# Block-causal attention and a gated MLP on one core: moves of turned P first on SyncE's queue, values loaded from ScalarE's queue, two diagonal copies on GpSimd

## The chip, the cores and the metric

The kernel runs on one core of one Trainium2 chip. The metric is the time of an execution on the device in microseconds (us); lower is better. Five engines are named as in the profile: PE (TensorE), DVE (VectorE), ACT (ScalarE), POOL (GpSimd) and SP (SyncE, which only issues transfers here). PEld is the loading of weights into PE. Transfers are also issued by ACT and POOL; an issuing engine's queue is shown as SPq, ACTq or as a DMA row of POOL.

## What is computed

Attention over 8 batches, 8 heads, 576 positions and 64 channels, with a mask of blocks of 64, and then a gated MLP over all 4608 rows of 512 features.

```python
scores = scale * np.matmul(q, k.transpose(0, 1, 3, 2))
mask = (pos[:, None] // 64) >= (pos[None, :] // 64)
scores = np.where(mask, scores, -1000000000.0)
scores = scores - np.max(scores, axis=-1, keepdims=True)
attn = np.exp(scores)
attn = attn / (np.sum(attn, axis=-1, keepdims=True) + 1e-09)
x = np.matmul(attn, v)            # then (B, H, S, D) -> (B * S, H * D)
...
gate = 1.0 / (1.0 + np.exp(-(x @ w_gate)))
val = x @ w_val
return (gate * val @ w_out).astype(np.float32)
```

All inputs are float32. Products that need more than one pass of PE's fast float format are made from a high and a low part (names in H and L).

## The kernel before, in words

**Stages.** The work runs over 32 pairs (a batch and two heads each, p = 0 to 31). Pairs 0 to 7 are laid out by a script (`FRONT`), in which every engine's order is written by hand. Pairs 8 to 31 run in a loop over p, in which the steps of table `REST` are written one after the other; a scheduler puts each engine's instructions into an order, within the limits that `behind` sets (an order between two instructions without a wait). Between the steps, `places` ticks deal out matmuls of the MLP's first part (`mlp`), which uses the rows of batches that are complete. After the loop comes the rest of the MLP, which the change does not touch.

**One pair.** Step `s` makes the scores of four row blocks into PSUM tiles named bank, and for each a maximum (nm, DVE) and two exps (ACT); `t` does the same for the last 64 rows (the tail). For pairs 8 to 30 (`moved`) exp writes P into a tile Z or XB, which take turns from pair to pair; both are called Zc. P must be transposed before it is multiplied with the values. DVE turns 32 x 32 blocks in place (`turn`, steps `tr3`, `tr2`, and the last and largest piece in `trm`). Step `trm` (`move`) then carries the blocks between the four groups of 32 partitions into tile G: twelve transfers of 100 KB, six issued by POOL and six by SP, and four copies on ACT for the blocks that stay in their group (the diagonal).

**The product with values** (`av`) of a pair is written into the next pair's loop pass, at step `AV`: 44 matmuls read G and the values VS, and DVE multiplies the result by rb, which gives xT. `finish` follows: XH (ACT), a store of xT to DRAM (ACT's queue) and XL (POOL). rb holds the reciprocals of the sums (step `r`, `recip`): DVE makes rT, four small transfers write it to DRAM (r_d), and three read it back over 64 partitions each (rb).

**Loads.** In pass p, steps `k` and `q` load pair p + 3 into tile rqk, four transfers of 72 KB each, and at the end of the pass the values of pair p + 2 are loaded into VS by three transfers. All go over SP's queue, as do r_d, rb and half of the moves. Step `k` also starts the preparation of the next pair (`prep`): DVE turns rqk into KQ, ACT makes KH and QH, POOL KL and the small copies QBH and QBL for the tail.

Names and lines before: `issue` L291 (its transfers are all L292), `load` L294, `turn` L580 (L583), `move` L585 (moves L589, copies L592), exps L486 and L530, xT L664, `finish` L788 (XH L790, store L793, XL L795), the loop L1193.

## Time and profile before

| what | before |
|---|---|
| median of 3 executions | 1152.83 us (1152.31 to 1154.24) |
| profiled execution | 1156.51 us, span 1154.7 us |
| PE busy | 1101.6 us, 95% of the span |
| DVE busy | 847.1 us, 73% |
| ACT busy | 621.6 us, 54% |
| POOL busy | 431.4 us, 37% |
| SP's transfers (q1) | 143.90 MB, 46.8% of 16 engines' span |
| granted PE clock, mean | 0.989 |

A busy PE is one with a matmul under way, whose end is modelled, so 95% does not say that PE works at its peak. The busy shares are means over stages that differ. SP has no busy time of its own in the profile; how full its queue is has to be read from its issues in order of time.

### The profile page before, as it was taken

The page shows a single profiled execution, that of the slowest core. Times are in us where ns is not written, and L with a number is a line of the kernel's source. Part 1 is how long each engine was busy: PE and PEld are TensorE (multiplying, and loading weights), DVE is VectorE, ACT ScalarE, POOL GpSimd, SP SyncE. Part 2 cuts the span into 40 slices and gives each one's busy share as a digit, 9 for nine tenths or more (in the row PEclk, how much of TensorE's full clock was granted, in tenths as well). Part 3 has the DMA queues.
Part 4 walks back from the last instruction along what each step waited for, and adds up shares of the span by engine and source line. Part 5 has one row for each costly group of instructions (what it writes and reads, how often), then busy time and mean ns, then how long its engine had stood idle before and what let it go on. Part 6 is the DMA issues. An engine that isn't in the chain of part 4 may idle for free.

```text
span 1154.7 us, 19512 instructions
## 1 busy us (share of the span) xinstructions
PE 1101.6 (95%) x6593; PEld 940.8 (81%) x6593; DVE 847.1 (73%) x1482; ACT 621.6 (54%) x1344; POOL 431.4 (37%) x560
## 2 busy tenths in 40 slices
PE   8999898988988998979999999999999999999998
PEld 6677676776766676767889999899899999998998
DVE  7999886776767677648869975776886665756754
ACT  6887776767767777744335354444553332422421
POOL 3655355444635555331011304213124243263250
PEclk9999999999999999999999999999999999999999
DMA  8797578778878887754412335505388345254351
GB/s 167 173 184 164 144 172 198 167 159 204 169 182 169 203 184 160 184 160 133 156 38 81 110 118 198 174 36 210 111 317 298 135 137 183 70 187 130 108 164 55
DMA packets 270691, 181.63 MB, mean 157 GB/s; under 512 B 204576, under 2 KB 225312, under 8 KB 269952
## 3 DMA queue, kind: packets, MB, share of 16 engines
q1 hardware_dynamic: 248080, 143.90, 46.8%
q10 hardware_dynamic: 17712, 21.30, 5.8%
q0 software_dynamic: 4800, 15.19, 5.5%
q8 instruction: 52, 0.85, 0.3%
q14 instruction: 47, 0.39, 0.1%
HBM read 104.73 MB, written 47.33 MB: 132 GB/s over the span
## 4 chain that ended last, share of the span: by engine, by line
PE 64%; DMA 11%; DVE 9%; SPq 6%; ACT 5%; issue 4%; POOL 1%; ACTq 0%; DVEq 0%; POOLq 0%
PE b L1250 30%; PE m L1320 11%; PE b L1320 6%; PE bank L347 5%; PE m L179 4%; SPq L292 4%; PE m L188 3%; PE bank L179 3%; ACT G L592 3%; DVE nm L474 2%; DMA G<-XB 2%; DMA rb<-r_d 2%; DMA r_d<-rT 2%; SPq L589 2%; DVE XB L583 1%
## 5 line engine op out<-in xcount | busy, mean ns | idle before, releaser
L1250 PE MATMUL b<-XH,w 128*128 128x384 f32 x1344 | 349.1, 335 | 0.3 <-ACT t L899 0.3
L1250 PEld LDWEIGHTS b<-XH,w 128*128 128x128 f32 x1344 | 243.8, 188 | 4.3 <-ACT t L899 0.7
L1250 PE MATMUL b<-XL,w 128*128 128x384 f32 x672 | 223.5, 335 | 0.0
L1250 PEld LDWEIGHTS b<-XL,w 128*128 128x128 f32 x672 | 126.1, 188 | 1.7
L347 PE MATMUL bank<-G,VS 128*64 128x64 f32 (+3 forms) x1264 | 103.6, 319 | 22.5 <-DMA r_d<-rT 9.4
L1320 PE MATMUL m<-wo,hH 128*128 128x512 f32 x368 | 119.9, 391 | 0.0
L347 PEld LDWEIGHTS bank<-G,VS 128*64 128x64 f32 x1264 | 73.2, 145 | 50.6 <-issue 14.0
L1069 POOL TENSOR_TENSOR XB<-XB 128x384 f32<-128x384 f32 x20 | 22.3, 1116 | 238.1 <-DMA XB<-xT_d 139.9
L188 PE MATMUL m<-wo,hH 128*128 128x512 f32 x256 | 85.7, 398 | 8.1 <-ACT ost L899 6.0
L1273 ACT ACTIVATE g<-g 128x384 f32<-128x384 f32 x72 | 37.9, 526 | 93.3 <-DVE g L1286 49.3
L179 PE MATMUL m<-XH,wg 128*128 128x512 f32 x240 | 81.5, 397 | 4.4 <-ACT t L203 4.4
L1082 ACT CAST XH<-XB 128x1536 fp32r<-128x1536 f32 (+2 forms) x72 | 65.1, 941 | 36.1 <-DVE XB L1080 23.5
L474 DVE TENSOR_REDUCE nm<-bank 128x2 f32<-128x1024 f32 (+1 forms) x96 | 77.0, 803 | 7.1 <-ACT Z L486 5.5
L179 PE MATMUL m<-XH,wv 128*128 128x512 f32 x240 | 81.7, 398 | 0.0
L1320 PEld LDWEIGHTS m<-wo,hH 128*128 128x128 f32 x368 | 69.0, 188 | 13.0
L1083 DVE TENSOR_TENSOR XL<-XB,XH 128x1536 fp32r<-128x1536 f32 (+2 forms) x72 | 75.8, 1085 | 0.0
L1320 PE MATMUL m<-wo,hL 128*128 128x512 f32 x184 | 72.1, 392 | 0.0
L1320 PE MATMUL b<-wo,hH 128*128 128x512 f32 (+1 forms) x216 | 71.5, 383 | 0.0
L486 ACT ACTIVATE Z<-bank,nm 128x512 f32<-128x512 f32 (+3 forms) x104 | 53.5, 530 | 30.8 <-DMA G<-XB 18.4
L389 POOL TENSOR_SCALAR KQ<-KQ 128x128 f32<-128x128 f32 x28 | 16.8, 601 | 131.7 <-DVE KQ L377 127.2
L188 PEld LDWEIGHTS m<-wo,hH 128*128 128x128 f32 x256 | 48.1, 188 | 20.9 <-ACT ost L899 8.1
L486 ACT ACTIVATE XB<-bank,nm 128x512 f32<-128x512 f32 (+3 forms) x88 | 45.4, 531 | 24.5 <-DMA G<-Z 13.6
(215 smaller groups left out, 2553.8 us busy)
## 6 DMA issues: line engine op xcount, KB each, us to landing
pr<-part_d SPq DMA_DIRECT2D x66, 256.0 KB
xT_d<-xT ACTq DMA_DIRECT2D x32, 288.0 KB
XB<-xT_d SPq DMA_DIRECT2D x16, 576.0 KB
part_d<-pr SPq DMA_DIRECT2D x36, 256.0 KB
rqk<-in_q_dram SPq DMA_DIRECT2D x120, 72.0 KB
rqk<-in_k_dram SPq DMA_DIRECT2D x120, 72.0 KB
out_dram<-pr SPq DMA_DIRECT2D x33, 256.0 KB
part_d<-ost ACTq DMA_DIRECT2D x32, 256.0 KB
```

What stands on the lines that cost most here:

```text
L179: mm = nc.tensor.matmul(ps, lhsT=lh, rhs=rh, start=(i == 0), stop=(i == n - 1))
L188: mm = nc.tensor.matmul(ps, lhsT=lh[:, f, t * P:(t + 1) * P], rhs=rh, start=(f == i == 0), stop=(f == F1 - 1 and i == 2))
L292: return pin(engine_of(queue), queue.dma_start(**kw), True)
L347: pe_last[:] = [pin("PE", nc.tensor.matmul(*args, **kw)).ins]
L474: mark("DVE", nc.vector.tensor_reduce(out=nm_()[:, c0:c0 + 2], in_=ps[:, :, c:c + n], axis=AX.X, op=ALU.max, negate=True))
L486: mark("ACT", nc.scalar.activation(out=dst, in_=src, func=AF.Exp, bias=nm_()[:, c0 + h:c0 + h + 1], accum_out=sm[:, 5 * h + i:5 * h + i + 1]))
L592: mark("ACT", nc.scalar.copy(out=Gc[q, c], in_=Zc[q, c]))
L1082: nc.scalar.copy(out=XO[j][0][:, a:b], in_=x)
L1083: sub = nc.vector.tensor_sub(out=XO[j][1][:, a:b], in0=x, in1=XO[j][0][:, a:b].bitcast(F32))
L1250: mm = nc.tensor.matmul(ps, lhsT=lh, rhs=rh, start=(first and k == 0), stop=(k == n - 1), skip_group_check=not first)
L1273: mark2("ACT", nc.scalar.activation(out=t, in_=c, func=AF.Tanh, scale=0.5))
L1320: mm = nc.tensor.matmul(po[t][:, cols], lhsT=lh[:, f, t * P:(t + 1) * P], rhs=wo[:, f, e, cols], start=((whole or half == 0) and i == 0), ...
```

## The change

Five edits go together.

- Six of the twelve moves are issued by SP as before, and are now marked; every later transfer that `issue` puts on SP's queue is placed behind the last marked move.
- Steps `k` and `q` no longer issue one load each: both loads are issued at step `q`, which is written behind `trm` and `r`.
- The loads of values go to ACT's queue.
- Of the four diagonal copies, two go to POOL, behind POOL's six moves.
- `finish` is a step of its own (`fin`) behind `trm` for passes 8 to 30; XH is placed behind ACT's last G copy and XL behind POOL's. The MLP matmuls of a completed batch are added at that step too.

```diff
--- before.py
+++ after.py
@@ -22,7 +22,7 @@
 AHEAD = 3
 KEEP = 32
 
-REST = (("s", 3), ("t", 1), ("AV", 2), ("tr3", 1), ("tr2", 1), ("k", 0), ("trm", 0), ("r", 0), ("q", 0), ("trl", 2), ("trt", 2))
+REST = (("s", 3), ("t", 1), ("AV", 2), ("tr3", 1), ("tr2", 1), ("k", 0), ("trm", 0), ("fin", 0), ("r", 0), ("q", 0), ("trl", 2), ("trt", 2))
 NB = 25
 B_OF = {2: (0, 3), 3: (6, 4), 0: (14, 1), 1: (16, 2)}
 LT = 14
@@ -289,7 +289,10 @@
         nc.gpsimd.memset(p_tile(4)[:, S:], 0.0)
 
         def issue(queue, **kw):
-            return pin(engine_of(queue), queue.dma_start(**kw), True)
+            ins = queue.dma_start(**kw)
+            if queue is nc.sync and "moves" in last:
+                behind(ins.ins, last["moves"])
+            return pin(engine_of(queue), ins, True)
 
         def load(p, what, queue=nc.sync, part=None):
             b, hp = pairs[p]
@@ -586,10 +589,15 @@
 
                 turn(LT, NB)
                 for k, (c, a) in enumerate(itertools.permutations(range(4), 2)):
-                    (nc.sync if k % 2 else nc.gpsimd).dma_start(out=Gc[32 * c:32 * c + 32, a], in_=Zc[32 * a:32 * a + 32, c])
+                    ins = (nc.sync if k % 2 else nc.gpsimd).dma_start(out=Gc[32 * c:32 * c + 32, a], in_=Zc[32 * a:32 * a + 32, c])
+                    mark("moves" if k % 2 else "POOL", ins)
                 for c in range(4):
                     q = slice(32 * c, 32 * c + 32)
-                    mark("ACT", nc.scalar.copy(out=Gc[q, c], in_=Zc[q, c]))
+                    if c % 2:
+                        ins = nc.gpsimd.tensor_copy(out=Gc[q, c], in_=Zc[q, c])
+                        behind(ins.ins, last["POOL"])
+                    else:
+                        mark("ACT", nc.scalar.copy(out=Gc[q, c], in_=Zc[q, c]))
 
             def tr_main(i):
                 if moved:
@@ -792,7 +800,10 @@
                     mark("ACT", cut)
                 nc.scalar.dma_start(
                     out=xT_d[b, hp * P:(hp + 1) * P, :], in_=xT_())
-                nc.gpsimd.tensor_sub(out=XL[:, hp], in0=xT_(), in1=XH[:, hp].bitcast(F32))
+                low = nc.gpsimd.tensor_sub(out=XL[:, hp], in0=xT_(), in1=XH[:, hp].bitcast(F32))
+                if "POOL" in last and p < len(pairs) - 2:
+                    behind(low.ins, last["POOL"])
+                    behind(cut.ins, last["ACT"])
 
             def step(what, is_fine=False, alt=False, queue=nc.sync):
                 if is_fine:
@@ -814,9 +825,10 @@
                     tr_low()
                 elif what == "trt":
                     tr_tail()
+                elif what == "fin":
+                    finish()
                 else:
                     av()
-                    finish()
 
             return step
 
@@ -1199,16 +1211,19 @@
                 if what == "AV":
                     if prev:
                         prev("av")
-                    if prev and what == "AV" and pairs[p - 1][1] == NP - 1:
-                        pb = pairs[p - 1][0]
-                        mlp = itertools.chain(mlp, mlp1(pb, mbank if p < n else bank))
-                        left += F1 * 6 * NC + 3 * F1 * 4
-                        rate = (left - KEEP) / (4 * TICKS)
-                elif what in "kq":
+                if what == ("fin" if N_FIRST < p < n - 1 else "AV") and prev:
+                    prev("fin")
+                    if pairs[p - 1][1] == NP - 1:
+                            pb = pairs[p - 1][0]
+                            mlp = itertools.chain(mlp, mlp1(pb, mbank if p < n else bank))
+                            left += F1 * 6 * NC + 3 * F1 * 4
+                            rate = (left - KEEP) / (4 * TICKS)
+                if what in "kq":
                     next(pr, None)
-                    if p + 3 < n:
-                        load(p + 3, what)
-                elif now:
+                    if what == "q" and p + 3 < n:
+                        load(p + 3, "k")
+                        load(p + 3, "q")
+                elif now and what not in ("AV", "fin"):
                     now(what)
                 for _ in range(places if now else 6 if what == "AV" else 0):
                     pe_ticks.append(pe_last[0])
@@ -1227,7 +1242,7 @@
                     early_work(p, tick)
             run(pr)
             if p + 2 < n:
-                load(p + 2, "v")
+                load(p + 2, "v", nc.scalar)
             prev = now
 
         s_at.close()
```

SyncE, one period of the loop before. rqk_92 and rqk_93 are the two tiles that k and q are loaded into; L589 are the moves.

```order
L589 DMA G<-Z 32x800 x6
L292 DMA r_d<-rT 9x32 x4
L292 DMA rqk_93<-in_q_dram 32x18x32 x2
L292 DMA rb<-r_d 64x576
L292 DMA rb<-r_d 64x64
L292 DMA rb<-r_d 64x512
L292 DMA rqk_93<-in_q_dram 32x18x32
L292 DMA VS_96<-in_v_dram 128x4x64 x2
L292 DMA VS_96<-in_v_dram 64x2x64
L292 DMA rqk_92<-in_k_dram 32x18x32 x4
L292 DMA rqk_92<-in_q_dram 32x18x32
```

The same period now, up to the next moves (L592):

```order
L592 DMA G<-Z 32x800 x6
L292 DMA r_d<-rT 9x32 x4
L292 DMA rqk_93<-in_k_dram 32x18x32 x2
L292 DMA rb<-r_d 64x576
L292 DMA rb<-r_d 64x64
L292 DMA rb<-r_d 64x512
L292 DMA rqk_93<-in_k_dram 32x18x32 x2
L292 DMA rqk_93<-in_q_dram 32x18x32 x4
L592 DMA G<-XB 32x800 x6
```

The loads of values have left the queue, and k and q of one pair stand together behind the moves and rb.

VectorE around the last turn of a pair before (128x4x352 is the last turn, sm, QL and rT belong to the same and the next pair, xT to the pair before):

```order
L377 STREAM_TRANSPOSE KQ<-rqk_93 128x576 x2
L583 STREAM_TRANSPOSE Z<-Z 128x4x352
L552 TENSOR_SCALAR sm_108<-sm_108 128x9
L664 TENSOR_TENSOR xT<-bank,rb 128x320
L664 TENSOR_TENSOR xT<-bank,rb 128x256
L396 SCALAR_TENSOR_TENSOR QL<-KQ,QH 128x448
```

The same place now:

```order
L380 STREAM_TRANSPOSE KQ<-rqk_93 128x576 x2
L672 TENSOR_TENSOR xT<-bank,rb 128x320
L672 TENSOR_TENSOR xT<-bank,rb 128x256
L586 STREAM_TRANSPOSE Z<-Z 128x4x352
L555 TENSOR_SCALAR sm_108<-sm_108 128x9
L399 SCALAR_TENSOR_TENSOR QL<-KQ,QH 128x448
```

xT of the pair before now stands ahead of the last turn. It does so in all 23 moved pairs; before it did in 2 of them.

ScalarE from the exps of a pair to its G copies now (L489 and L533 are the exps, L533 that of the tail, L385 and L390 make KH and QH, L600 are the G copies):

```order
L489 ACTIVATE Z,sm_108<-bank,nm 128x2x4x32 x2
L214 CAST hH<-h_3340 128x512
L489 ACTIVATE Z,sm_108<-bank,nm 128x4x32 x2
L292 DMA VS_96<-in_v_dram 64x2x64
L533 ACTIVATE Z,sm_108<-bank,nm 128x4x160
L292 DMA VS_96<-in_v_dram 128x4x64
L385 CAST KH<-KQ 128x576
L292 DMA VS_96<-in_v_dram 128x4x64
L390 ACTIVATE QH<-KQ 128x448
L801 DMA xT_d<-xT 128x576
L203 ACTIVATE t<-m 128x512
L600 COPY G<-Z 32x800 x2
```

Three loads of values stand among the exps and casts, the first ahead of the tail's exp, and two copies are left where four were.

## Rows read from the trace of the kernel before

**Rows 1.** Busy time by stage; each engine's busy us (instructions), granted clock, DMA share, GB/s.
```profile
0.00:150.00 150.00, 139.94 (x952) 103.12 (x954) 129.21 (x240) 116.84 (x310) 76.04 (x106) 0.99 0.77 169
150.00:500.00 350.00, 316.59 (x2288) 247.46 (x2287) 259.32 (x446) 249.23 (x588) 180.56 (x296) 0.98 0.80 181
500.00:1154.70 654.70, 645.04 (x3357) 590.20 (x3355) 458.57 (x797) 255.56 (x447) 174.77 (x159) 0.99 0.43 142
```
**Rows 2.** Timeline of SyncE's issues: start us, us, engine, line, transfer, count [idle before <-releaser].
```profile
131.23 3.98 SPq L589 DMA_DIRECT2D G<-Z  x6
...
229.48 5.86 SPq L589 DMA_DIRECT2D G<-Z  x6
...
413.57 5.21 SPq L589 DMA_DIRECT2D G<-XB  x6
418.88 1.72 SPq L292 DMA_DIRECT2D r_d<-rT  x4
420.65 0.87 SPq L292 DMA_DIRECT2D rqk<-in_q_dram  x2
422.06 1.76 SPq L292 DMA_DIRECT2D rb<-r_d  x3
423.87 0.59 SPq L292 DMA_DIRECT2D rqk<-in_q_dram  x1
424.50 1.75 SPq L292 DMA_DIRECT2D VS<-in_v_dram  x3
426.34 2.29 SPq L292 DMA_DIRECT2D rqk<-in_k_dram  x4
428.72 0.56 SPq L292 DMA_DIRECT2D rqk<-in_q_dram  x1
429.39 4.57 SPq L589 DMA_DIRECT2D G<-Z  x6
...
492.36 4.12 SPq L589 DMA_DIRECT2D G<-Z  x5
```
**Rows 3.** Timeline of VectorE: last turns (128x1408) and xT.
```profile
243.38 0.82 DVE L664 TENSOR_TENSOR xT<-bank,rb 128x320 f32<-128x320 f32 x2 [1.69 <-DMA rb<-r_d]
...
424.03 1.65 DVE L583 STREAM_TRANSPOSE Z<-Z 128x1408 f32<-128x1408 f32 x1
...
439.69 1.60 DVE L583 STREAM_TRANSPOSE XB<-XB 128x1408 f32<-128x1408 f32 x1
...
442.29 0.82 DVE L664 TENSOR_TENSOR xT<-bank,rb 128x320 f32<-128x320 f32 x2 [0.46 <-DMA rb<-r_d]
```
**Rows 4.** Timeline of TensorE: the product with values of two pairs.
```profile
421.45 2.97 PE L347 MATMUL bank<-G,VS 128*64 128x256 f32 x44 [0.70 <-ACT Z L486]
...
436.43 2.97 PE L347 MATMUL bank<-G,VS 128*64 128x256 f32 x44 [0.56 <-DMA G<-Z]
```
**Rows 5.** Busy time in stretches of one period (columns as in rows 1).
```profile
420.00:426.00 6.00, 5.30 (x57) 4.34 (x56) 6.00 (x8) 4.31 (x15) 1.85 (x2) 1.00 0.42 96
...
429.40:435.00 5.60, 5.60 (x39) 4.41 (x38) 3.65 (x8) 3.96 (x11) 3.45 (x5) 1.00 1.09 259
```
**Rows 6.** ScalarE: a group of 165:500, an issue's timeline row, and a wait of 165:500.
```profile
L592 ACT COPY G<-Z 32x800 f32<-32x800 f32 x41 | 35.2, 859 | 10.4 <-DMA rb<-r_d 4.1 <-DVE Z L583 2.9 <-PE m L188 1.5
...
101.53 0.39 ACTq L292 DMA_DIRECT2D VS<-in_v_dram  x1
...
ACT G L592 <- DMA rb<-r_d: 4.1, 3, 1.9
```
**Rows 7.** GpSimd: timeline of one period, and its groups by form over the span.
```profile
426.70 3.02 POOL L589 DMA_DIRECT2D G<-Z  x6
429.77 0.51 POOL L402 CAST QBL<-QL 64x64 fp32r<-64x64 f32 x2
...
L773 POOL CAST XH<-xT 128x576 fp32r<-128x576 f32 x4 | 3.1, 776 | 0.0
```

## The prediction, made before the change was run

> **What bounds the kernel now.** I read the stages first, since the change touches one of them. Pairs 8 to 30 of the 32 (batch, head pair) items turn P by moves; that stretch lies between 131 and 500 us. There TensorE is busy 316.6 of 350 us, ScalarE and VectorE about three quarters, and the DMA engines have a share of 0.80; behind 500 us nothing of the change runs [rows 1]. No compute engine is full, so I looked for who makes whom wait.
>
> The second view is SyncE's own queue over one period [rows 2]. From 413.57 to 429.39 us, 15.82 us, SyncE issues six moves (5.21), four r_d stores (1.72), two q loads (0.87), three rb loads (1.76), one q load (0.59), three v loads (1.75), four k loads (2.29) and one q load (0.56). That is 14.75 us of 15.82: **the issue queue of SyncE is full**. The blocks of moves begin at 131.23 and at 492.36 us, with 21 blocks between them, so 22 periods have a mean of 361.1 / 22 = 16.41 us.
>
> What the full queue costs is seen on VectorE [rows 3]. The last turn of a pair ends at 425.68 (424.03 + 1.65); from then on its moves could start. GpSimd starts its six at 426.70 [rows 7], SyncE only at 429.39, after v, k and q. TensorE begins the product with values at 436.43, 7.0 us behind SyncE's first move, and its idle time ended with G<-Z [rows 4]. So SyncE's half is **3.7 us late**, and the product waits for it.
>
> How does lateness become time? The chain runs from a pair's scores over exp, turn, moves and the product with values to the scores of the pair two places on, because TensorE keeps its order. It spans two periods, so 3.7 us in it is worth at most 1.85 us a period: 16.41 - 1.85 = 14.56. TensorE's own work sets a like floor: from 421.45 to 436.43 is 14.98 us with 0.56 idle [rows 4], so 14.4.
>
> **The change part by part.** *v loads to ScalarE.* SyncE loses 1.75 us a pair and keeps 13.0, less than the floor, so it stops being full. ScalarE gains three issues; one took 0.39 there early in the program [rows 6], so 1.2 us.
> *k and q after the moves.* The issues are the same in number; the 2.29 + 0.56 us that stood ahead of SyncE's moves now stand behind r_d and rb. A load has two pairs' time until its tile is read, so I cost this at nothing; without that cover a transpose of rqk would wait and the turn behind it.
> *Two diagonal copies to GpSimd.* ScalarE loses 2 x 0.859 = 1.72 [rows 6], which pays for the 1.2. The trace has no such copy on GpSimd. Its copy of 576 columns takes 0.776 [rows 7], so 800 columns by length 1.08, from 0.86 (ScalarE's time) to perhaps twice 1.08; I take 1.08, as the row is the same kind of work. Two end 1.0 + 3.0 + 2.2 = 6.2 us behind the turn, while the moves issued beside them need about 7: hidden. At twice that, they end at 8.4 and the product waits 1.4 more. The copy of QBL behind them on GpSimd comes 2.2 us later than at 429.77 [rows 7]; that is 432 here, and the tail scores that read it ran at about 435.
> *The finish moved behind the move step.* XH, XL and the store of xT come after the G copies or just ahead of them. XH and XL are read only once a batch is complete. The MLP's next batch joins four ticks later, some 12 matmuls, and KEEP leaves 32 in stock: nothing.
> *A wait that the diff doesn't show.* The order of VectorE changes: the two products that make xT of the pair before stood behind the last turn in 21 of 23 pairs, and now stand ahead of it in all 23. xT needs rb, which comes from r_d, which SyncE issues behind the moves of the pair before. So a ring closes in one period: **moves, r_d, rb, xT, turn, next moves**. Before, from SyncE's first move to the start of xT took 12.90 us (429.39 to 442.29) or 13.90 (229.48 to 243.38), both times with rb as what ended the idle time [rows 2, 3]. Add xT 0.82 and the turn 1.60 [rows 3]: 15.3 to 16.3, with hand-overs 15.4 to 16.4. The upper value is today's period.
>
> What shortens the ring: the six issues took 4.57 and 5.86 in these two cases and 3.98 in the first block, before the queue was full [rows 2]. With 13.0 us of issues in a longer period SyncE will wait for the turn rather than the turn for SyncE, and I expect its six moves to go out in about 4 us: 0.6 to 1.9 less, so 14.5 to 14.8. What lengthens it: both halves now start together, 2.7 us apart before, and while SyncE's half ran the DMA share was already 1.09 against 0.42 just before the loads [rows 5]. I give back 0.4 to 0.7 and take a period of **15.2 us**. The gain is (16.41 - 15.2) x 22 = 26.6 us. The profiled execution took 1156.5 us (span 1154.7), 3.7 above the median of 1152.8; from the median that leaves **1126.2 us**. The forecast's own range is a period of 14.6 to 15.8, so 1113 to 1139.
>
> DMA: Bandwidth & Descriptors of the Trainium skill, section "Issuing engines are not separate DMA queues", says that transfers of all issuers share the same 16 engines, so that another issuer saves only issue time, usually a small thing. By that alone the sum would stay at 1153. Here the issue time is the full resource, and the share of 0.42 between the moves and the next loads [rows 5] says that the engines are not.
>
> **The rivals.** *TensorE's floor:* the ring shrinks below 14.5 and all lateness goes; 14.4 x 22 is 44 us less, 1109. For it: SyncE's 13.0 and the two-period chain's 14.56. Against: xT now stands in the turn's way. Chance 0.15.
> *The wait takes another's place:* rb comes as late as now, the ring stays at 16.4, and SyncE's idle time is all that is won; 1153, between 1146 and 1158. The same results if the DMA engines are what the moves wait for (share 0.80 over the stage, over 1 during moves): then the moves land when they land now. For it: the 13.90 case. Against: both cases were measured with a full queue. Chance 0.17 (0.06 of it faster, 0.08 the same, 0.03 slower).
> *ScalarE is held up, and the kernel is slower:* its DMA issues wait in line like any instruction. Before, its G copies were held three times, up to 1.9 us, until rb landed [rows 6], with one or two DMAs a pair on its queue. Now there are three more, and the first v load stands ahead of the tail's exp, which the last turn reads. If that costs 1.9 us in every pair, the period is 17.1 and the kernel takes 1153 + 0.7 x 22 = 1168. It decides from 1.2 us a pair on, which is what the forecast wins. Against: the place is early in the period, when the transfers ahead should have landed. Chance 0.13.
>
> **How the numbers follow.** The forecast has 0.55. I call the same what lies within 0.2% (2.3 us), about what a measurement of this kernel can tell. Faster: 0.55 + 0.15 + 0.06 = 0.76; the same 0.08; slower 0.03 + 0.13 = 0.16. The range goes from 1106, a little below the floor's time, to 1155; the slower cases lie outside it.
>
> **What would show it.** Right: SyncE's moves start within a microsecond of the turn's end and of GpSimd's; SyncE has idle time ahead of them; the blocks of moves are 15.2 us apart; xT waits for rb and the turn follows at once. Wrong: a period above 16 with xT's idle time ended by rb (the ring), or ScalarE's exp or cast idle behind a v load (the slower rival). If SyncE's moves still start 3 us late, the change doesn't do what it says. If the period is under 14.6, rb came sooner than I think.

## The result and the profile after

The changed kernel took **1167.77, 1169.66 and 1170.74 us**, against a median of 1152.99 us for the kernel before, run beside it on the same chip. A fourth execution took 1345.86 us at a granted clock of 0.753 instead of 0.987 to 0.988 and is left out of the ratio; the recorded median of 1170.2 us counts it. The ratio is **1.0141, with a 95% interval of 1.0121 to 1.0161**: it is slower by about 16 us. The forecast was 1126.2 us with a range of 1106 to 1155. The time moved the other way.

The profiled execution took 1170.74 us, with a span of 1168.9. Its busy times by stage, in the columns of [rows 1], are:

```profile
0.00:150.00 150.00, 138.45 (x939) 100.89 (x940) 127.60 (x236) 110.61 (x302) 72.89 (x97) 0.98 0.74 163
150.00:500.00 350.00, 310.94 (x2182) 241.09 (x2181) 245.08 (x430) 208.55 (x526) 214.86 (x330) 0.98 0.77 175
500.00:1168.90 668.90, 661.31 (x3476) 603.47 (x3474) 473.38 (x819) 265.24 (x472) 191.26 (x181) 1.00 0.43 143
```

Between 150 and 500 us TensorE runs 2182 matmuls instead of 2288 [rows 1]: this stage goes slower, and what it did not reach is done behind it.

SyncE's timeline after, with the columns of [rows 2], shows the first and last blocks of moves and one whole period:

```profile
131.42 4.44 SPq L592 DMA_DIRECT2D G<-Z  x6
...
423.51 4.77 SPq L592 DMA_DIRECT2D G<-XB  x6
428.37 1.93 SPq L292 DMA_DIRECT2D r_d<-rT  x4
...
432.51 1.77 SPq L292 DMA_DIRECT2D rb<-r_d  x3
...
439.77 2.44 SPq L592 DMA_DIRECT2D G<-Z  x4
...
509.79 4.42 SPq L592 DMA_DIRECT2D G<-Z  x6
```

From 131.42 to 509.79 there are again 22 periods: 378.37 / 22 = **17.20 us** against 16.41 before. The difference, 0.79 x 22 = 17.4 us, is all of the loss and a little more: the two profiled executions are 14.2 us apart (spans of 1168.9 and 1154.7), and from the last block of moves to the end the changed kernel takes 659.1 us instead of 662.3. So the question is what makes a period longer, although the moves are no longer late. VectorE's rows of the same period show both:

```profile
421.80 1.65 DVE L586 STREAM_TRANSPOSE XB<-XB 128x1408 f32<-128x1408 f32 x1 [0.91 <-ACT XB L533]
...
435.28 0.82 DVE L531 TENSOR_REDUCE nm<-bank 128x1 f32<-128x640 f32 x1 [2.83 <-PE bank L350]
436.02 1.43 DVE L380 STREAM_TRANSPOSE KQ<-rqk 128x576 f32<-128x576 f32 x2
437.38 0.78 DVE L672 TENSOR_TENSOR xT<-bank,rb 128x320 f32<-128x320 f32 x2
438.08 1.62 DVE L586 STREAM_TRANSPOSE Z<-Z 128x1408 f32<-128x1408 f32 x1
```

The last turn ends at 423.45 (421.80 + 1.65) and SyncE's moves start at 423.51; the next turn ends at 439.70 and the moves start at 439.77. The 3.7 us of [rows 2, 3] are gone. But the maximum of the tail's scores (L531) has waited 2.83 us for TensorE. Over 165 to 490 us such waits come to

```profile
DVE nm L531 <- PE bank L350: 52.7, 19, 6.5
DVE bank L508 <- PE bank L350: 32.0, 19, 2.8
DVE xT L672 <- DMA rb<-r_d: 2.3, 5, 0.8
```

(total us, times, longest us), that is 52.7 us in 19 waits, of a kind that VectorE's waits before don't have at all. What TensorE does instead is in its own order. Before (the same stretch as the second line of [rows 4]):

```profile
434.91 0.31 PE L347 MATMUL bank<-KH,QBH 128*128 128x320 f32 x1
...
435.59 0.28 PE L347 MATMUL bank<-KL,QBH 128*128 128x256 f32 x1
436.43 1.28 PE L347 MATMUL bank<-G,VS 128*64 128x256 f32 x15 [0.56 <-DMA G<-Z]
```

After:

```profile
429.42 0.39 PE L350 MATMUL bank<-KH,QBH 128*128 128x320 f32 x1
432.35 2.05 PE L350 MATMUL bank<-G,VS 128*64 128x256 f32 x26 [2.54 <-DMA r_d<-rT]
434.32 0.41 PE L350 MATMUL bank<-KH,QBL 128*128 128x320 f32 x1
...
434.96 0.28 PE L350 MATMUL bank<-KL,QBH 128*128 128x256 f32 x1
435.18 1.32 PE L350 MATMUL bank<-G,VS 128*64 128x128 f32 x18
```

Before, six matmuls make the tail's scores and then the 44 of the product with values of the pair before follow. After, one of the six comes first, then TensorE waits for the moved G, runs 26 matmuls of the product, and only then the other five of the tail. (The waits put down to r_d there are for G: the product reads no r_d, and by the trace's semaphores the last of GpSimd's moves landed at 431.65 and the last of SyncE's at 432.00.) So the scores of pair p stand behind the product of pair p - 1, which needs the moves of pair p - 1, and **a ring closes in one period**: moves, product, tail scores, their maximum, their exp, last turn, next moves. Here it has 8.84 us from the first move to the product, 1.97 to the second tail matmul, 0.96 to the maximum, 1.26 to the exp on ScalarE (its row is below), 1.54 to the turn, 1.62 for the turn and 0.07 to the move: 16.26 us, this period. Before, the tail's scores stood ahead of the product and waited for no move of the pair before.

```profile
435.87 0.62 ACTq L292 DMA_DIRECT2D VS<-in_v_dram  x1
436.54 0.80 ACT L533 ACTIVATE Z<-bank,nm 128x640 f32<-128x640 f32 x1 [3.25 <-PE bank L350]
```

At its end this ring has two ways from the maximum to the turn. Over ScalarE, a load of values is issued ahead of the exp (first row), and the exp ends at 437.34. VectorE itself has no idle time from the maximum on: KQ's two turns (1.43 us) and xT (0.78) fill it until the last turn starts at 438.08, so in this period the turn waits for VectorE and not for the exp. xT is new in this place. From the end of the maximum to the start of the turn the mean is 2.39 us (18 pairs between 165 and 490 us, xT in between in all of them), against 1.55 before (19 pairs, in none).

GpSimd's rows tell where the order comes from. QBL, which the second tail matmul reads, stands on GpSimd behind the moves, and now behind the two copies as well:

```profile
424.74 3.03 POOL L592 DMA_DIRECT2D G<-XB  x6
427.82 1.75 POOL L597 COPY G<-XB 32x800 f32<-32x800 f32 x2
429.63 0.53 POOL L405 CAST QBL<-QL 64x64 fp32r<-64x64 f32 x2
```

At run time QBL is there at 430.16, over 4 us before the matmul that reads it (434.32). The matmul waits for its place in the order, not for QBL. That a scheduler which sees QBL come later puts the product first is the theory; the experiments below test it.

### The profile page after: what moved, and what is told of

The parts are those of the page before. It is cut to its first block, busy times and chain, and to the rows that moved or that the text cites. A ratio compares the mean times of both kernels' runs of the same rounds, so it can differ in the third digit from the quotient of the medians.

```text
span 1168.9 us, 19634 instructions
## 1 busy us (share of the span) xinstructions
PE 1110.7 (95%) x6593; PEld 945.4 (81%) x6593; DVE 846.1 (72%) x1482; ACT 584.4 (50%) x1298; POOL 479.0 (41%) x606
## 4 chain that ended last, share of the span: by engine, by line
PE 73%; DMA 9%; DVE 6%; SPq 5%; issue 2%; ACT 2%; POOL 1%; ACTq 0%; DVEq 0%; POOLq 0%
PE b L1265 30%; PE m L1335 11%; PE bank L350 11%; PE b L1335 6%; PE m L179 6%; PE m L188 6%; SPq L292 5%; PE bank L179 3%; DMA r_d<-rT 2%; DVE nm L477 2%; DMA rb<-r_d 1%; DMA rqk<-in_k_dram 1%; DMA VS<-in_v_dram 1%; DMA rqk<-in_q_dram 1%; PE bank L188 1%
## 5 line engine op out<-in xcount | busy, mean ns | idle before, releaser
L350 PE MATMUL bank<-G,VS 128*64 128x64 f32 (+3 forms) x1264 | 110.8, 322 | 41.4 <-DMA rqk<-in_k_dram 18.5
L350 PEld LDWEIGHTS bank<-G,VS 128*64 128x64 f32 x1264 | 78.1, 145 | 71.4 <-issue 25.1
L1335 PEld LDWEIGHTS m<-wo,hH 128*128 128x128 f32 x368 | 69.0, 188 | 13.0
L489 ACT ACTIVATE Z<-bank,nm 128x512 f32<-128x512 f32 (+3 forms) x104 | 53.5, 530 | 30.6 <-DVE nm L477 10.3
L392 POOL TENSOR_SCALAR KQ<-KQ 128x128 f32<-128x128 f32 x28 | 16.9, 603 | 121.7 <-DVE KQ L380 121.7
L531 DVE TENSOR_REDUCE nm<-bank 128x1 f32<-128x640 f32 x23 | 18.9, 823 | 62.1 <-PE bank L350 62.1
L1329 POOL TENSOR_TENSOR pr<-pr,pr 128x512 f32<-128x512 f32 x33 | 43.7, 1329 | 39.1 <-DMA pr<-part_d 26.5
```

The source lines that it names most:

```text
L350: pe_last[:] = [pin("PE", nc.tensor.matmul(*args, **kw)).ins]
L489: mark("ACT", nc.scalar.activation(out=dst, in_=src, func=AF.Exp, bias=nm_()[:, c0 + h:c0 + h + 1], accum_out=sm[:, 5 * h + i:5 * h + i + 1]))
L1329: nc.gpsimd.tensor_add(out=pr[t], in0=pr[t], in1=other)
L1335: mm = nc.tensor.matmul(po[t][:, cols], lhsT=lh[:, f, t * P:(t + 1) * P], rhs=wo[:, f, e, cols], start=((whole or half == 0) and i == 0), ...
```

## The experiments

Theory A is the ring above. The mean period of each run is taken as before: the first and last of 23 blocks of SyncE's moves, divided by 22. All ratios are to the kernel before, run beside it. A period comes from one profiled execution; the executions of the kernel before lie between 1149.5 and 1161.3 us, which is 0.5 us a period, so smaller differences of periods are not told apart by the table's last column alone. In tail_first and some runs built on it the last of the 23 pairs keeps the woven order.

| run | tail's scores stand | ratio (95% interval) | period, us |
|---|---|---|---|
| before | ahead of the product | 1 | 16.41 |
| the change | woven into it | 1.0141 (1.0121 to 1.0161) | 17.20 |
| tail_first | ahead | 0.9985 (0.9963 to 1.0008) | 16.30 |
| copies_act | ahead | 1.0069 (1.0038 to 1.0100) | 16.73 |
| v_sp | woven | 1.0135 (1.0100 to 1.0170) | 17.25 |
| tail_late | behind | 1.0754 (1.0717 to 1.0792) | 20.53 |
| pool_only | woven | 1.0291 (1.0253 to 1.0328) | 18.14 |
| moves_only | ahead | 1.0018 (1.0000 to 1.0036) | 16.63 |
| tf_pool4 | ahead | 1.0056 (1.0033 to 1.0080) | 16.26 |
| tf_vsp | ahead | 1.0029 (1.0014 to 1.0043) | 16.72 |
| qbl_dve | ahead | 1.0018 (0.9999 to 1.0037) | 16.40 |
| tf_qpool | ahead | 0.9980 (0.9957 to 1.0003) | 16.25 |
| tf_ostdve | ahead | 1.0031 (1.0009 to 1.0052) | 16.57 |
| tf_qbl_qpool | ahead | 1.0197 (1.0168 to 1.0225) | 17.44 |
| tf_both | ahead | 1.0005 (0.9987 to 1.0022) | 16.41 |
| be_light | ahead | 0.9902 (0.9865 to 0.9939) | 16.58 |
| tf_light | ahead | 1.0000 (0.9978 to 1.0021) | 16.38 |
| after_light | woven | 1.0131 (1.0110 to 1.0151) | 17.37 |
| tf_p1 | ahead | 1.0187 (1.0149 to 1.0225) | 16.94 |
| be_p1 | ahead | 1.0009 (0.9987 to 1.0030) | 16.48 |

### First question: is it the order on TensorE?

**tail_first** adds one order to the changed kernel, without a wait: in `s_tail_moved` the last tail matmul is noted, and in `av` the product's first is put behind it.

```diff
+                    last[f"tail{i}"] = pe_last[0]
...
+                            if i == j == h == 0:
+                                for e in range(2):
+                                    if f"tail{e}" in last:
+                                        behind(pe_last[0], last[f"tail{e}"])
```

> The changed kernel with one order added on TensorE: the six matmuls of the moved tail's scores stand ahead of the first matmul of the previous pair's product with values, as they did before the change; in the changed kernel five of them stand behind its 26th matmul. Theory A (tail scores woven into the product close a ring: moves, product, tail scores, maximum, last turn, next moves): the ring is cut, the 5 us for which VectorE's maximum of the tail waits for TensorE go, and with SyncE's moves still on time the mean distance between blocks of moves falls from 17.2 us to 14.6 to 15.5, 1110 to 1135 us in all. Theory B (GpSimd's two copies cost by their own length and place): the order on TensorE changes nothing, 1165 to 1175 us. Theory C (the loads of values hold ScalarE up): also 1165 to 1175 us. Theory D (the product's factor read back from memory, which now ends ahead of the last turn, closes the ring): 1165 to 1175 us if that order stays, and a gain if it goes.

Measured: 0.9985, so the 1.4% are gone, and nothing is won beyond that. Theories B and C (GpSimd's copies or ScalarE's loads by themselves) fall as the cause of the loss. Theory D does not fall by this run, because with the tail first xT stands behind the last turn again, in 22 of 23 pairs. It falls by the changed kernel's own waits: there xT waits for rb 2.3 us in all, in 5 waits (third line of VectorE's waits above). VectorE's largest wait for TensorE is again the one for the first scores of a pair, and the one for the tail is no longer among its waits. But the 1110 to 1135 us which theory A promised with it did not come; that is the second question.

**copies_act** is the change with all four diagonal copies on ScalarE:

```diff
-                    if c % 2:
-                        ins = nc.gpsimd.tensor_copy(out=Gc[q, c], in_=Zc[q, c])
-                        behind(ins.ins, last["POOL"])
-                    else:
-                        mark("ACT", nc.scalar.copy(out=Gc[q, c], in_=Zc[q, c]))
+                    mark("ACT", nc.scalar.copy(out=Gc[q, c], in_=Zc[q, c]))
```

> The changed kernel with all four diagonal copies on ScalarE, as before the change; SyncE's order and the loads of values on ScalarE's queue stay. Here the six tail score matmuls stand ahead of the product again. Theory A (tail scores woven into the product): 1110 to 1140 us, close to the run with the order alone forced, later by up to 1 us a period for the two copies of some 0.86 us on ScalarE. Theory B (GpSimd's copies): about the same, 1110 to 1140, so this run alone does not part A from B. Theory C (loads of values on ScalarE): ScalarE is now fuller by 1.7 us a period, 1165 us or more.

Measured: 1.0069, 1164 us, above what theory A gave and just under theory C's bound. Without copies on GpSimd the tail stands ahead of the product by itself, and half of the loss goes. The rest comes where ScalarE has both all copies and the loads: with all the copies and no loads there (moves_only, below) it is 1.0018, with the loads and half of the copies 0.9985 (tail_first).

**v_sp** puts the loads of values back on SyncE (`load(p + 2, "v")`), and nothing else.

> The changed kernel with the loads of values back on SyncE's queue, behind the moves; GpSimd keeps two copies and the tail scores stay woven into the product (five of six behind its 26th matmul). Theory A: the ring is as long as in the changed kernel, 1165 to 1178 us. Theory C (loads on ScalarE's queue hold its exponentials up): at or below the kernel before, 1120 to 1153 us. Theory B: as in the changed kernel, 1165 to 1175 us.

Measured: 1.0135, 17.25 us, as slow as the change. The loads on ScalarE's queue don't make the loss. They do hold the tail's exp up: in the changed kernel it starts 0.23 to 2.51 us behind the end of its maximum, a mean of 1.04 over 18 pairs, with a load issued in between each time, and in v_sp 0.04. But VectorE's turns of KQ and xT cover most of that: from the maximum to the turn it takes 2.39 us in the changed kernel and still 2.23 in v_sp.

**tail_late** makes the kernel before worse in one point: in `REST` the step `AV` is written ahead of `t`, which with one more order puts all six of the tail's matmuls behind the whole product.

```diff
-REST = (("s", 3), ("t", 1), ("AV", 2), ("tr3", 1), ("tr2", 1), ("k", 0), ("trm", 0), ("r", 0), ("q", 0), ("trl", 2), ("trt", 2))
+REST = (("s", 3), ("AV", 2), ("t", 1), ("tr3", 1), ("tr2", 1), ("k", 0), ("trm", 0), ("r", 0), ("q", 0), ("trl", 2), ("trt", 2))
...
+                        if (i or k) and "av26" in last:
+                            behind(pe_last[0], last["av26"])
```

> The kernel before the change with one thing altered: the tail's six score matmuls are written behind the previous pair's product with values, and stand behind all of it on TensorE; SyncE's order, the loads and the copies are those of before. Theory A: the same ring closes in the old kernel, and there SyncE's moves still come 3.7 us late, so it must be longer than the 17.2 us of the changed kernel: 18 to 21 us a period, 1185 to 1255 us. Theories B and C (GpSimd's copies or ScalarE's loads make the loss): no such loss here, 1150 to 1160 us.

Measured: 1.0754 and 20.53 us, as theory A said. TensorE runs the product (429.53) and some of the feed-forward part, then the tail (436.13); the maximum waits:

```profile
429.53 5.16 PE L347 MATMUL bank<-G,VS 128*64 128x256 f32 x44 [4.24 <-DMA r_d<-rT]
436.13 0.32 PE L347 MATMUL bank<-KH,QBH 128*128 128x320 f32 x1
```

```profile
437.14 0.82 DVE L530 TENSOR_REDUCE nm<-bank 128x1 f32<-128x640 f32 x1 [1.56 <-PE bank L347]
...
439.23 1.60 DVE L585 STREAM_TRANSPOSE XB<-XB 128x1408 f32<-128x1408 f32 x1
```

SyncE's order was not touched here, yet its next moves start at 441.26, 0.43 us behind the turn: with the turn itself late, SyncE has time for all the rest. Lateness of SyncE and lateness of the turn replace one another. xT stands in none of the 16 pairs between the maximum and the turn here, so the order on TensorE makes a loss without it.

**pool_only** is the kernel before with the two copies on GpSimd (the lines removed in copies_act) and nothing else.

> The kernel before with the two diagonal copies on GpSimd and nothing else of the change. This edit by itself turns the order on TensorE from six tail matmuls ahead of the product into one, then 26 of the product, then the other five. Theory A (that order closes the ring of moves, product, tail, maximum, last turn): 17.2 us a period or more, since SyncE is not helped here, 1165 to 1195 us. Theory E, formed after the first runs (the woven order costs, but only because SyncE's transfers were put in another order as well): 1150 to 1160 us.

Measured: 1.0291, 18.14 us. This edit alone turns the order on TensorE, as its rows show:

```profile
449.01 0.39 PE L347 MATMUL bank<-KH,QBH 128*128 128x320 f32 x1
451.99 2.05 PE L347 MATMUL bank<-G,VS 128*64 128x256 f32 x26 [2.60 <-DMA r_d<-rT]
453.97 0.41 PE L347 MATMUL bank<-KH,QBL 128*128 128x320 f32 x1
```

It costs 2.9%, and theory E falls. The full change costs 1.4%: within this ring the rest of the change, the timely moves above all, is worth 18.14 - 17.20 = 0.94 us a period, a part of it by TensorE's clock (last section).

**qbl_dve** is the change with QBL's copies on VectorE instead of GpSimd, and no order forced:

```diff
-                            pin("POOL", nc.gpsimd.tensor_copy(out=x[rows(h), h], in_=src[rows(h), S - P - D:]))
+                            eng = "DVE" if x is QBS[1] and p > N_FIRST else "POOL"
+                            pin(eng, (nc.vector if eng == "DVE" else nc.gpsimd).tensor_copy(
+                                out=x[rows(h), h], in_=src[rows(h), S - P - D:]))
```

> The changed kernel with the pair of small copies that make QBL taken from GpSimd, where they stand behind the moves and the two diagonal copies, to VectorE, where QL is made; no order is forced on TensorE. The six tail matmuls then stand ahead of the product by themselves. Theory A (QBL's place behind GpSimd's copies is what turned the order, and the order is what cost): as fast as the kernel before or faster, 1135 to 1155 us. If the order forced by hand was only hiding another fault of the change, about 1160 us or more.

Measured: 1.0018, 16.40 us. All three parts of the change are in it, and the tail stands ahead of the product in all the periods read. With pool_only this settles the cause: **the two copies ahead of QBL on GpSimd turned the order on TensorE, and that order makes the loss.** How the loss divides between the tail behind the product and xT ahead of the turn is not parted: the change, v_sp and pool_only have both, tail_first and qbl_dve neither.

### Second question: why do timely moves win nothing?

**moves_only** keeps SyncE's order alone: copies_act with the loads of values back on SyncE.

> The changed kernel without its loads on ScalarE and without its copies on GpSimd: SyncE's order alone is left of the change. Tail scores ahead of the product. Theory A alone would have SyncE's timely moves pay here: 1125 to 1145 us. Theory F, formed after the run with the order forced on TensorE gave no more than the old time (SyncE's lateness was covered: ScalarE's copies wait for the last turn, the evictions of the feed-forward layers stand behind them, and TensorE waits for those): the time stays within half a per cent of before, 1148 to 1160 us, with TensorE's waits for the tiles ost and t on ScalarE as long as in the kernel before or longer.

Measured: 1.0018, inside theory F's range. The moves start 1.0 to 5.2 us behind the turn, so SyncE's queue is still full. Even so TensorE's idle time ahead of the product falls from a mean of 0.92 us (17 pairs before, 212 to 480 us) to 0.26, and in 9 of 17 pairs it has none. The last move lands a mean of 1.2 us ahead of the product (0.4 before), so G is there in time. TensorE's idle time a period does not fall: 1.6 before, 1.8 here. copies_act shows the same with SyncE's moves a mean of 0.4 us behind the turn: the last move lands 1.7 us ahead of the product, which has no idle time ahead of it in 12 of 15 pairs, and the period is no shorter. **With the old order on TensorE and G there in time, an earlier G wins nothing**; these two runs show it.

**tf_vsp** is tail_first with the loads of values back on SyncE.

> The changed kernel with the tail's scores forced ahead of the product and the loads of values back on SyncE's queue. It tells what the loads on ScalarE's queue are worth where the order on TensorE is the old one. Theory F: ScalarE gets 1.2 to 1.7 us of issuing a period back, ahead of its evictions, so 1140 to 1150 us; if instead SyncE's queue is still what limits, the moves come later again and it is 1155 to 1165 us.

Measured: 1.0029, 1156.9 us and 16.72 us, which is where the expectation put a queue of SyncE that still limits. SyncE's moves come 2.2 to 6.3 us behind the turn, in tail_first 0.1 to 2.9, and TensorE's idle time ahead of the product is 1.29 us instead of 0.72. The loads on ScalarE are worth 0.2 us a period there by the ratios, 0.4 by the profiled executions.

**tf_qpool** is tail_first with `load(p + 3, "q", nc.gpsimd)`. It frees SyncE.

> The changed kernel with the tail's scores forced ahead of the product and the four loads of q a period on GpSimd's queue instead of SyncE's. Theory G (SyncE's queue still bounds: its rows filled 14.9 of 16.3 us a period in the run with the order forced, and the moves came up to 2.9 us after the turn): SyncE loses 2.2 us a period, the moves follow the turn at once, the period falls by 0.4 to 0.8 us, 1130 to 1144 us. Theory F (ScalarE's evictions bound): 1147 to 1156 us. The four issues cost GpSimd some 2 us a period, beside 10 us of other work.

Measured: 0.9980, with an interval that holds 1: theory G's 1130 to 1144 us did not come. SyncE's, GpSimd's, VectorE's and TensorE's rows of one period:

```profile
405.04 3.91 SPq L593 DMA_DIRECT2D G<-XB  x6
...
421.75 1.82 SPq L593 DMA_DIRECT2D G<-Z  x3
```

```profile
405.18 0.74 POOL L292 DMA_DIRECT2D rqk<-in_q_dram  x1 [1.12 <-PE bank L350]
...
407.32 1.98 POOL L292 DMA_DIRECT2D rqk<-in_q_dram  x3
...
410.37 2.98 POOL L593 DMA_DIRECT2D G<-XB  x6
```

```profile
403.37 1.60 DVE L587 STREAM_TRANSPOSE XB<-XB 128x1408 f32<-128x1408 f32 x1
```

```profile
415.21 0.31 PE L350 MATMUL bank<-KH,QBH 128*128 128x320 f32 x1
...
418.17 2.97 PE L350 MATMUL bank<-G,VS 128*64 128x256 f32 x44 [1.99 <-ACT hH L214]
```

The turn ends at 404.97 and SyncE's moves start at 405.04; in 16 of the 17 pairs read the distance is 0.1 us or less, and SyncE's rows fill 11.9 us of a period of 16.3. But the loads of q now stand ahead of GpSimd's own moves, which start at 410.37, 5.40 us behind the turn. Between 212 and 480 us GpSimd's half starts a mean of 4.2 us behind the turn (2.2 in tail_first, 1.4 before) and is the last to land in all 16 pairs. In the rows above TensorE has done the tail by 416.17 and idles 1.99 us ahead of the product; SyncE's half had landed at 413.48, GpSimd's at 417.46. (The wait is put down to hH, which the product does not read.) So the condition of theory G, moves that follow the turn at once, came for one half only, and the other half took the lateness over. SyncE's half alone is not what bounds this version. Whether both halves together are, with the order forced, this run does not decide.

**tf_pool4** is tail_first with all four copies on GpSimd; **tf_ostdve** is tail_first with the evictions `ost` of the middle batches on VectorE; **tf_both** joins tf_ostdve and tf_qpool.

```diff
-            pin("ACT", nc.scalar.mul(out=ost, in_=po, mul=0.5))
+            if 0 < b < B - 1:
+                pin("DVE", nc.vector.tensor_scalar_mul(ost, po, 0.5))
+            else:
+                pin("ACT", nc.scalar.mul(out=ost, in_=po, mul=0.5))
```

> The changed kernel with the tail's scores forced ahead of the product (as in the run before) and all four diagonal copies on GpSimd, so that nothing on ScalarE waits for the last turn but the exponentials. Theory F (evictions queued behind ScalarE's copies hold TensorE up): TensorE's waits for ost and t, some 14 us on its matmuls between 165 and 490 us, mostly go, and the period falls by 0.4 to 0.8 us, 1130 to 1144 us. Against it (GpSimd's copies come later, each 0.85 us, and the product waits for them): no gain or a loss, 1150 to 1165 us, with TensorE waiting for G on GpSimd.

> The changed kernel with the tail's scores forced ahead of the product and the evictions of the second feed-forward product (ost) of all batches but the first and last on VectorE instead of ScalarE. Theory F (those evictions stand behind ScalarE's waits for the last turn and hold TensorE up): TensorE's waits for ost go, 1130 to 1146 us. Theory G (SyncE's queue): no gain, 1148 to 1160 us, the more so as VectorE gets 0.8 us or so more a period.

> The changed kernel with the tail's scores forced ahead of the product, the loads of q on GpSimd's queue and the evictions ost of the middle batches on VectorE. Each by itself took one kind of TensorE's waits away and another came. Together, if the waits add up: TensorE's idle time falls under 1 us a period, 1130 to 1145 us. Theory T with idle time that only changes places: 1147 to 1160 us.

Measured: 1.0056, 1.0031 and 1.0005. tf_pool4 has a period 0.04 us under tail_first's and is slower all the same, by time behind the last block of moves (670.5 us instead of 660.5); the cause stays open. In tf_ostdve TensorE's waits for ost fall from 14.0 us (the lines of tail_first below) to 3.2, and its waits put down to r_d, which are those for G, rise from 7.5 to 22.9. What is taken from one place appears at another, and theory F, that those evictions are the bound, falls. tf_both has GpSimd's half late as in tf_qpool, a mean of 4.2 us.

**tf_qbl_qpool** joins tail_first, qbl_dve and tf_qpool.

> The changed kernel with the tail's scores forced ahead of the product, QBL's copies on VectorE and the loads of q on GpSimd's queue: all that the first runs suggest for SyncE and the tail together. Theory G: 1125 to 1142 us, faster than the kernel before. If TensorE's fixed order and ScalarE are what is left, 1142 to 1156 us.

Measured: 1.0197, 1179.59 us, far above both forecasts. Its periods have TensorE waiting for t, h and ost, and not for G (0.20 us ahead of the product); why these three edits together lose what none of them loses was not settled.

**be_light, tf_light and after_light** shorten every third matmul of the feed-forward part's first product from 512 to 128 columns, in the kernel before, in tail_first and in the changed kernel. (The low part of x is left out of 384 columns of that product.)

```diff
+                cols = P if i % 3 == 1 else rh.shape[-1]
-                mm = nc.tensor.matmul(ps, lhsT=lh, rhs=rh, start=(i == 0), stop=(i == n - 1))
+                mm = nc.tensor.matmul(ps[:, :cols], lhsT=lh, rhs=rh[:, :cols], start=(i == 0), stop=(i == n - 1))
```

> The kernel before with 128 instead of 512 columns in every third matmul of the feed-forward layers' first product (the pass with the low part of x; its result is left out for the other 384 columns). That takes some 7.6 x 0.17 = 1.3 us of TensorE's work out of a period and leaves every wait and transfer. Theory T (TensorE's full round sets the period): 16.4 falls by 0.9 to 1.4 us. Rival R (a chain of latencies through scores and turn): it falls by under 0.4 us, and TensorE idles more.

> The same lighter feed-forward matmuls in the changed kernel with the tail's scores forced ahead of the product. Theory T: 16.3 falls by 0.9 to 1.4 us as in the kernel before, and no more than 0.3 us better than there, if SyncE's timely moves are worth nothing; if they are worth something as soon as TensorE has room, it falls by more than the kernel before does, to 14.6 or less. Rival R: under 0.4 us.

> The same lighter feed-forward matmuls in the changed kernel as it is. Theory A (its 17.2 us are a chain: moves, product, tail scores, maximum, last turn): TensorE's work is mostly not what the chain waits for, so the period falls by less than in the other two, 0 to 0.6 us, to 16.6 to 17.2. If TensorE's work sets this kernel's period too, 0.9 to 1.4 us.

Measured: periods of 16.58, 16.38 and 17.37 us, none shorter than in the heavier kernels (16.41, 16.30, 17.20). What be_light wins, 0.9902, lies behind the last block of moves: 1140.9 - 496.0 = 644.9 us to its end, against 1154.7 - 492.4 = 662.3. In tf_light the same matmuls win only 1.2 us there (659.3 against 660.5); why is open. Inside the stretch of moves TensorE's busy time a period falls by 0.4 to 0.5 us and not by 1.3 (14.77 to 14.31, 14.68 to 14.27, 15.23 to 14.80), while the granted clock falls from 0.98 to 0.95 in the first two pairs of runs and from 0.97 to 0.96 in the third (150 to 490 us). Its idle time grows by as much or more (1.64 to 2.27, 1.63 to 2.11, 1.97 to 2.56). Theory T, that TensorE's work sets the period, would have shortened it by those 0.4 us at least; it falls for all three at that size. TensorE's waits of 165 to 490 us in tail_first:

```profile
PE m L179 <- ACT ost L916: 8.7, 5, 3.2
...
PE m L188 <- ACT ost L916: 5.3, 5, 2.2
...
PE m L179 <- ACT t L203: 1.7, 2, 1.4
```

and in tf_light, where those lines of the kernel are one further down:

```profile
PE m L180 <- ACT ost L917: 11.2, 5, 3.1
PE m L180 <- ACT t L204: 8.6, 4, 2.3
...
PE m L189 <- ACT ost L917: 5.5, 5, 1.6
```

The lighter matmuls wait longer for ScalarE to clear their banks: 25.3 us instead of 15.7.

**tf_p1 and be_p1** test one chain for that, in tail_first and in the kernel before: last turn, ScalarE's evictions behind it, the 24 feed-forward matmuls between product and next scores, scores, maxima, last turn. Twelve of the 24 are moved:

```diff
-REST = (("s", 3), ("t", 1), ("AV", 2), ("tr3", 1), ("tr2", 1), ("k", 0), ("trm", 0), ("fin", 0), ("r", 0), ("q", 0), ("trl", 2), ("trt", 2))
+REST = (("s", 5), ("t", 3), ("AV", 2), ("tr3", 1), ("tr2", 1), ("k", 0), ("trm", 0), ("fin", 0), ("r", 0), ("q", 0), ("trl", 0), ("trt", 0))
```

> The changed kernel with the tail's scores forced ahead of the product, and with four of the twelve places a period at which feed-forward matmuls are put on TensorE moved from behind the last turns to behind the scores and the tail: 12 instead of 24 feed-forward matmuls stand between the product and the next scores, about 14 (12 before) between scores and tail, about 10 (none before) between tail and product. Theory R (the chain goes from the last turn over ScalarE's evictions and those feed-forward matmuls to the next scores; the product itself is not in it): turn to scores falls from 5.4 us by 1.5 to 2.7, the period to 14.5 to 15.5, 1115 to 1140 us. If TensorE's round is only dealt otherwise: 16.0 to 16.5 us, 1145 to 1160. If the product is in the chain after all, it comes later and the period grows over 16.6.

> The kernel before with the same places moved: 12 instead of 24 feed-forward matmuls between product and next scores, 20 between scores and tail, 4 between tail and product. Theory R: the period falls from 16.4 too, by less, since 8 more of them stand between scores and tail and SyncE's moves come late, to 15.2 to 16.2 us, 1128 to 1150 us. If TensorE's round is only dealt otherwise, 1150 to 1160 us.

Measured: 1.0187 and 1.0009. Theory R's time did not come in either; in tf_p1 the period grew over 16.6, as was expected if the product is in the chain. In tf_p1 the periods scatter, from 13.87 to 21.67 us between 208 and 502 us. TensorE's rows of one of 20.83 us (254.51 to 275.34) show how:

```profile
263.89 0.28 PE L350 MATMUL bank<-KL,QBH 128*128 128x256 f32 x1
...
264.71 0.39 PE L188 MATMUL m<-wo,hH 128*128 128x512 f32 x1
268.23 0.50 PE L188 MATMUL m<-wo,hH 128*128 128x512 f32 x1 [3.13 <-ACT ost L916]
...
272.31 2.97 PE L350 MATMUL bank<-G,VS 128*64 128x256 f32 x44
```

The feed-forward matmuls that now stand between tail and product wait 3.13 us for ScalarE, and the product, whose G has long been moved, stands behind them in the same queue. In such a period the chain was not cut but led through the product.

**What stays open.** With the tail ahead of the product, the period is 16.2 to 16.7 us in every version but tf_qbl_qpool and tf_p1 (17.4 and 16.9). Excluded as its sole bound are SyncE's half of the moves (tf_qpool), the eviction ost on ScalarE (tf_ostdve) and TensorE's busy time, as far as it was cut (tf_light). No run with the order forced has both halves of the moves early, so in those versions the landing of G is not excluded. What the runs suggest, without showing it, is that TensorE's fixed order ties scores, evictions and product into one round, in which each saving is waited for elsewhere. No version that does all the work beats the kernel before by more than its interval; the best are tf_qpool and tail_first.

## Why the prediction was wrong

**The step that failed** stands in the part on GpSimd's copies: QBL "comes 2.2 us later than at 429.77 [rows 7]; that is 432 here, and the tail scores that read it ran at about 435". It was costed at nothing since QBL would still be in time. In time it was (430.16 in the period shown), but the order on TensorE had been made from expected times, and in that order five tail matmuls went behind 26 of the product. With it a period is 0.79 us longer in the whole change and 1.73 in pool_only; the old order forced back (tail_first) ends the loss. The orders of SyncE, VectorE and ScalarE were compared, that of TensorE was not. So the path was wrong too: the ring that limits goes over the product, the tail's scores and their maximum (16.26 us in the period shown), and the forecast's ring over r_d, rb and xT, on which its 15.2 us stood, did not bind.

**The second step that failed** is the worth of SyncE's lateness: "SyncE's half is 3.7 us late, and the product waits for it", "at most 1.85 us a period". The lateness was real and it went. But the same [rows 4] showed how long TensorE idled ahead of the product: 0.56 and 0.70 us, a mean of 0.92 over the 17 pairs. An earlier G by itself can take away no more idle time than that, 0.92 x 22 = 20 us. Of these, moves_only took 0.66 us a period away and won nothing, as TensorE waited elsewhere.

**Point by point:**
- *SyncE stops being full.* Right in the changed kernel: its rows fill 13.3 us of 17.2, where 13.0 was forecast, and six moves take a mean of 4.3 us, where "about 4" was. With the old order forced (tail_first) it is 14.9 of 16.3, since six moves take 6.2 us there. The rows also hold waits between issues: before, they fill 15.0 of 16.4 us, the issues alone 14.0.
- *Loads of values on ScalarE cost nothing.* Right for the change (v_sp). The rival that ScalarE is held up gave 1168 us, close to the 1170.2, but it is not what made the loss. Its sign did come: in the row above ScalarE's exp idled 3.25 us, the first 2.8 for TensorE's tail and the maximum and the last 0.4 behind a load, a mean of 1.04 us from maximum to exp. It cost little, as VectorE was not ready for the turn either, and v_sp, without it, is as slow.
- *Copies on GpSimd of 1.08 us each.* 0.88 measured (1.75 for two), and hidden as such; what they pushed back was not.
- *k and q behind the moves, the finish moved.* Right for the tiles: VectorE's turns of rqk do not show up as waiting for a load. But the cost was not nothing for the queue: q's loads now stand just ahead of the next moves, and between 165 and 490 us SyncE's moves wait for loads of q to land for 5.5 us in 8 waits in the changed kernel and 23.1 us in 36 in tail_first; before, it was 2.4 us in 5, for loads of k.
- *The ring through rb and xT.* VectorE's xT does stand ahead of the last turn, but the row at 437.38 has no idle time ahead of it, and xT's waits for rb come to 2.3 us in all. The ring does not bind; the 15.2 us that rested on it had no ground. What xT's new place does is add its own 0.78 us between the maximum and the turn of the ring that binds. It goes with the order on TensorE and not with the moved finish: pool_only has it without that edit.
- *The rule of DMA: Bandwidth & Descriptors* (the Trainium skill, "Issuing engines are not separate DMA queues"), by which another issuer saves little and the sum stays at 1153, was set aside because SyncE's queue was full. It came out near that with the old order on TensorE: tail_first, with v on ScalarE's queue, 0.9985, and tf_qpool, with q on GpSimd's besides, 0.9980. That a queue is full does not say how long anyone waits for its end.
- *TensorE's floor of 14.4 us* was never reached; in tf_light TensorE's busy time fell by 0.4 us a period and the period did not.

## What to carry to other kernels

Where a scheduler makes the orders, an operation that is moved onto an engine also moves what stands behind it there, and can turn the order of a third engine that reads it; compare the orders of every engine before costing the move, the fullest one first. A late transfer is worth at first no more than the idle time that its reader shows ahead of reading it, however late it is by its issuer's queue. A transfer that is moved to another queue makes late what stands behind it there (GpSimd's moves in tf_qpool), so read every half of a set of transfers, not only the one that was to be helped. And where idle time only changes its place under several cures, look at the order that ties the waits together next.

## What the runs showed of the hardware

TensorE's clock fell behind its own idle time, which made the slow periods slower. Two stretches of the changed kernel, each beginning with the product's 26 matmuls, in the columns of [rows 1]:

```profile
346.50:351.00 4.50, 4.42 (x34) 3.19 (x36) 0.05 (x1) 0.81 (x4) 0.00 (x0) 0.66 0.56 151
432.30:436.50 4.20, 4.15 (x50) 3.36 (x50) 1.37 (x3) 0.81 (x4) 0.96 (x1) 1.00 0.47 112
```

In the first TensorE had idled 2.78 us, the granted clock was 0.66 of full speed, so partly at the lower of its two levels (1.2 and 2.4 GHz), and the 26 took 3.49 us. In the second it had idled 2.54, the clock was full, and they took 2.05. In tail_late the whole product took 5.16 us behind 4.24 us of idle time, instead of 2.97. A wait of TensorE can so cost more than its length. The length of the last wait alone does not decide it: in pool_only the clock was 0.55 of full speed (340.7 to 344.5) behind 1.63 us of idle time, ahead of which TensorE had idled 0.34 us once more. Over the stretch of moves the granted clock is 0.98 before, 0.97 in the changed kernel, 0.94 in pool_only and 0.89 in tail_late, so a part of what the last two lose is the clock's.

A block of SyncE's issues is no fixed price: six moves took a mean of 4.2 us in tail_late (16 blocks, 3.74 at the least) and 6.2 in tail_first (20 blocks, 165 to 490 us). The price of one issue is the same in both, a median of 0.59 us, though single ones reach 1.6 and 2.0. Most of the difference is waiting between the issues, 0.2 us a block in tail_late and 1.5 in tail_first, there above all for loads of q to land:

```profile
SPq L593 <- DMA rqk<-in_q_dram: 23.1, 36, 1.7
```
